# Attention into a mixture of experts and a gated layer: G's transfers moved to GpSimd's queue, XW written by VectorE, gate work re-ordered within a chunk

## The chip, the cores and the metric

The kernel runs on one core of one Trainium2 chip. Its time is the device time of one execution in microseconds. Before the change the median of three runs is 1039.93 us (1037.31 to 1040.97). The core's engines have queues of their own and meet at semaphores: TensorE (PE, matrix products into PSUM; PEld loads its weights), VectorE (DVE), ScalarE (ACT), GpSimd (POOL) and SyncE (SP). DMAs are issued from SP's queue (the profile calls it hardware_dynamic) and from GpSimd's (software_dynamic). Each queue is worked in order.

## The reference

Three layers follow one another, on 3072 tokens of 384 features (4 batches of 768 steps; 8 heads of 48).

```python
# 1: attention with a delta rule, state is 48x48 per batch and head
k_n = k / (norm(k) + 1e-6)
for t in range(768):
    y[:, :, t] = q_t @ state
    state = state + beta_t * outer(k_t, v_t - k_t @ state)
# 2: mixture of 8 experts, one per token
e = argmax(x @ w_gate); p = softmax(x @ w_gate)[e]
out = p * sigmoid(x @ w_output_gate)[e] * (relu(x @ w1[e]) @ w2[e])
# 3: gated layer
y = (sigmoid(x @ w_gate2) * (x @ w_val)) @ w_out
```

## The kernel before, in words

The kernel runs the layers as three stages. The first, attention, takes until about 304 us; the experts follow until about 570, and the gated layer until the end. The gate of the second layer (which expert each token gets, and its place in the list of that expert) is worked out during the first stage, for the tokens already finished, and their rows are scattered to the list `disp` in device memory by indirect DMAs on GpSimd's queue (`scatter`, L513).

The attention cuts the 768 steps into 12 chunks of 64, worked for all 32 pairs of batch and head at once. Inside a chunk the recurrence becomes a triangular system, solved in two halves of 32 rows with inverses of 32 x 32 blocks. Two chunks form a group, and a group's inverses are formed together: ScalarE copies the products of keys to `G` (diagonal blocks of a chunk's first half, rows of the tile `GD`) and to `GS`; two DMAs per chunk bring the second half's blocks from `GS` into `G` (`gp_evac`, L258; `G<-GS`). VectorE transposes `G` to `Lt` (`prep`), normalises, and builds the inverse `X` column by column (`inv_ops`: pairs of `tmp<-X,Lt` and `X<-X,tmp`). For groups 1 to 5 GpSimd does rows 16 to 30 of it (15 pairs `tmpG<-X,Lt`, `X<-X,tmpG`). The last step, `last`, transposes `X` to `XT`. Products need half of XT on other partitions; that is `XW` (`x_swap`, L271; `XW<-XT`).

The loop over chunks (L623 and after) then runs, for chunk c: the state read `KU<-SH,KQ` on TensorE; VectorE's first `W<-VT,KU`; the products with the inverse, `KU<-W,XT` and `KU<-W,XW` (64 small matmuls); ScalarE's copy `UF<-KU`; `KU<-UF,GS`; VectorE's second W; the inverse's products again; UF again; the state's update `Sps<-UF,KH`; and ScalarE's copy of the state to `SH`, from which the next chunk starts. Chunk 0 has no state, and its first products take `VT` in place of W. Beside this chain TensorE makes the products of keys for chunk c + 5 (`gp_mm`, `GY<-KQ`, in two halves), the output (`y_mm`: `GY<-SH,KQ`, and then `GY<-UF,PM`), and the gate's work on finished rows: transposes `XTP<-cst,XG` (`gate_t`), logits `GL<-wgo,xt` (`gate_l`, twice a chunk), and in odd chunks the places in the lists, `GL<-g_oh` and `GL<-acc,ones` (`gate_r`). VectorE does the small operations between them (`gate_v1`, `gate_e`, `gate_v2`).

VectorE's order is written out beforehand. `Filler` (L88) keeps a list of the inverse's steps (its main chain) and of side chains, each operation with an assumed duration. `fil.run(TA)` puts filler of a budget of TA between a chunk's first and second W, `fil.run(TB)` between the second W and the next chunk's first; `fil.add` hangs operations beside the main chain, `fil.flush(chain)` runs the filler until that chain is out, and the plain `flush(ops)` writes the operations out at once. At the end of an odd chunk the filler runs until the next group's inverse is done. `share_rows` hands out GpSimd's rows. SP's order is that of the code: at a chunk's end it loads V and K for chunk c + 2 (`VT`, `kt`, 8 transfers each), and fills part of `disp` with zeros.

Of the kernel before, what the change touches and what calls it, by code (L numbers as in the profile page):

```python
# [13 lines left out]
ALU = mybir.AluOpType  # L14
# [7 lines left out]
NSTEP, NG = SEQ // CH, SEQ // CH // 4  # L22
# [13 lines left out]
LA = 5  # L36
# [8 lines left out]
TC = 9.5  # L45
NR = 16
SHE = (0, 16, 16, 16, 16, 16)
TA = 6.0
TB = 11.0
TB0 = 11.0  # L50
W0 = 36
YS = 69
# [77 lines left out]
class Attention:  # L130
# [5 lines left out]
    def run(self, small, acc, zero_fill, small_loads):  # L136
# [121 lines left out]
        def gp_evac(c, k, ps):  # L258

            hs = slice(4 * k, 4 * k + 4)  # L260
            A.copy(out=gd(c)[:, :, hs], in_=ps[:, :, :, 0:32])
            A.copy(out=GS[c % RP][:, :, hs], in_=ps[:, :, :, 32:64])
            A.copy(out=PM[c % RP][:, :, hs], in_=ps[:, :, :, 64:128])
            if k:
                g, c2 = divmod(c, 2)
                for x in range(2):
                    SP.dma_start(
                        out=GD[g][quad(x, 1), 16 * c2 : 16 * c2 + 16].rearrange("p m t -> p (m t)"),
                        in_=GS[c % RP][quad(x, 1)].rearrange("p r h t -> p (r h t)"))

        def x_swap(g):  # L271
            x4 = XTS[g % 2].rearrange("p (c r h) t -> p c r (h t)", c=2, r=2)
            for x in range(2):
                o, i = XTW[g % 2][half(x)].rearrange("p c h t -> p c (h t)"), x4[half(1 - x), :, 1]
                if g:
                    SP.dma_start(out=o, in_=i)
                else:
                    V.tensor_copy(out=o, in_=i)

        def xt(c, h, b, i):  # L280

# [40 lines left out]
            sc = [(0.6, 0.0, lambda: scale(0, 16)), (0.33, GAP, lambda: scale(16, 32))]  # L322
            return ops, sc

        others, fresh = [], []

        def share_rows(n):
            for f in others[:n]:
# [4 lines left out]
        def inv_ops(g, share=32):  # L333

            X = ep.tile([128, 32, 32], F32, tag="X", name="X", bufs=2)

            def zero():
                (A if g else G).memzero(X.rearrange("p k i -> p (k i)")) if g else G.memset(X, 0.0)

            def diag(F):  # L340
                F.cut[g % 2] = 0
                if g:
                    others.extend(other)
                V.tensor_scalar_mul(out=X.rearrange("p k i -> p (k i)")[:, 0:1024:33], in0=nbr[:, g], scalar1=-1.0)
                F.t += 0.085
                F.ready = F.t + GAP

            def mul(E, j, k0, k1):
                n, m = k1 - k0, 31 - j
                tag, w = ("tmpG", 160) if E is G else ("tmp", 256)  # L350
                t = ep.tile([128, w], F32, tag=tag, name=tag, bufs=2)[:, : n * m].rearrange("p (a b) -> p a b", a=n)
                E.tensor_tensor(out=t, in0=X[:, k0:k1, j : j + 1].to_broadcast([128, n, m]), in1=LT[g][:, j : j + 1, j + 1 : 32].to_broadcast([128, n, m]), op=ALU.mult)
                return t

            def add(E, j, k0, k1, t):
                E.tensor_tensor(out=X[:, k0:k1, j + 1 : 32], in0=X[:, k0:k1, j + 1 : 32], in1=t, op=ALU.add)

            dur = lambda n, j: 0.095 + n * (31 - j) / 980

            def col(j):  # L360
                n = min(j + 1, share)

                def second(F, parts):
                    for k0, k1, t in parts:
                        add(V, j, k0, k1, t)
                        F.t += dur(k1 - k0, j)
                    F.ready = F.t + (GAP if len(parts) == 1 else 0.02)

                def first(F):
                    split = F.idle(F.t + dur(n, j)) and n * (31 - j) >= 100  # L370
                    if n // 2 - F.cut[g % 2] > CUT or not 0 < F.cut[g % 2] < n:
                        F.cut[g % 2] = n // 2
                    h = F.cut[g % 2]
                    ks = [(0, h), (h, n)] if split else [(0, n)]
                    parts = []
                    for k0, k1 in ks:
                        parts.append((k0, k1, mul(V, j, k0, k1)))
                        F.t += dur(k1 - k0, j)
                    F.ready = F.t + (0.0 if split else GAP)
                    if split:  # L380
                        second(F, parts)
                    else:
                        F.main.insert(0, lambda F: second(F, parts))

                return first

            def last(F):
                share_rows(99)
                V.transpose(out=XTS[g % 2].rearrange("p k i -> p i k"), in_=X.rearrange("p k i -> p i k"))
                F.t += 1.9  # L390
                F.ready = F.t
                F.done = g
                if g:
                    fresh.append(g)
                if g == 0:
                    V.memset(zl, 0.0)

            other = [(lambda j=j: add(G, j, share, j + 1, mul(G, j, share, j + 1))) for j in range(share, 31)]
            return zero, other, [diag] + [col(j) for j in range(31)] + [last]
# [6 lines left out]
        def GL(g):  # L406
            if not GLB:
                GLB.append(gp_.tile([128, 512], F32, tag="GL", name="GL", bufs=1))
            return GLB[0][:, 128 * (g % 2) : 128 * (g % 2) + 128]
# [92 lines left out]

        late = small["late"]

        def late_rows():

            tot = GL(NG - 1)[:, 96:97]
            raw_mm(out=tot, lhsT=ones, rhs=acc[:, 0:1], start=True, stop=True)
            V.tensor_scalar(out=late[:, 0:1], in0=tot, scalar1=-1.0, scalar2=float(E0), op0=ALU.mult, op1=ALU.add)
            V.tensor_scalar_max(out=late[:, 0:1], in0=late[:, 0:1], scalar1=0.0)  # L510
            V.tensor_copy(out=late[:, 1:8], in_=eoff[:, 1:8])

# [87 lines left out]
        ahead(3, ("GY", "KU"))  # L600
        ahead(4, ("GY", "KU"))
        k_turn(0)
        x_swap(0)
        ops, sc1 = prep(1)
        load_kq(LA + 1)
        for e in (1, 2):
# [16 lines left out]
        for c in range(NCH):  # L623
# [4 lines left out]
                early.close()  # L628

            beside(c, "load", engines)  # L630
            while fresh:
                x_swap(fresh.pop(0))
            S0, vp = SH, VT[c]
            KU = two("KU")
            KUv = KU[:, :, 0:384].rearrange("p r (h e) -> p r h e", h=8)
# [2 lines left out]
            Wv = W.rearrange("p r (h e) -> p r h e", h=8)  # L638
            sv = lambda b, h: S0[rows(b), pos(b), 48 * h : 48 * h + 48]

            def y_mm():
                for h, b in hb:
                    mm(out=Yp[half(pos(b)), par(b), 48 * h : 48 * h + 48], lhsT=kq(c, 1, h, b), rhs=sv(b, h), start=(h == 0), stop=False)

            if c > 0:
# [6 lines left out]
                    mm(out=KU[:, r, 0:384], lhsT=SHz[:, r, 0:128], rhs=SHz[:, r], start=True, stop=False)  # L652
                W1 = vp.rearrange("p r (h e) -> p r h e", h=8)
            if c % 2 == 1 and c > 1:
                fil.flush(fil.add(gate_v1(g - 1)))
            if more:
                P = gp_mm(c + LA, 0, "GY", mm)
            elif c > 0:
                Yp = two("GY")
                y_mm()  # L660
            beside(c, "KS", engines)
            if c > 0 and c + RK - 1 < NCH:
                load_kq(c + RK - 1)

            for h, b in sorted(hb, key=lambda x: par(x[1])) if c == 0 else hb:
                mm(out=KUv[quad(opp(b), 0), par(b), h], lhsT=xt(c, h, b, 0), rhs=W1[quad(pos(b), 0), par(b), h], start=True, stop=True)
            if c > 0:
                fil.run(TA)
            share_rows(NR // 2)
# [3 lines left out]
            if not last:  # L673
                v_mul(c + 1, (0,), A)
                vm = fil.add([(0.5, 0.0, lambda c=c: v_mul(c + 1, (1,), V))])
            if c % 2 == 1 and c > 1:
                gate_r(g - 1, mm)
                v2 = gate_e(g - 1) + gate_v2(g - 1)
            if c > 0:
                gate_t(2 * c - 2)  # L680
            if last:
# [2 lines left out]
                mm(out=KUv[quad(pos(b), 1), par(b), h], lhsT=GS[c % RP][quad(opp(b), 0), par(b), h], rhs=UF[quad(opp(b), 0), par(b), h], start=False, stop=False)  # L684
            V.tensor_tensor(out=W, in0=vp, in1=KU[:, :, 0:384], op=ALU.subtract)
            if c % 2 == 1 and c > 1:
                fil.flush(fil.add(v2))
                if last:
                    for j in range(2 * c - 6, 2 * c - 2):
                        scatter(j)  # L690
            if more:
                P = gp_mm(c + LA, 1, "GY", mm)
            if c > 0:
                gate_l(2 * c - 2, mm)
            if last:
                beside(c, "V", engines, Sps[:, 1])
            for h, b in hb:
# [3 lines left out]
            if more:  # L701
                gp_evac(c + LA, 1, P)
            if c > 0:
                gate_t(2 * c - 1)
            if not last:
                for h, b in hb:
                    mm(out=Sps[rows(b), pos(b), 48 * h : 48 * h + 48], lhsT=KH[c][half(opp(b)), par(b), h], rhs=UF[half(opp(b)), par(b), h], start=False, stop=False)
                SH = wk.tile([128, 2, 384], F32, tag="SH", name="SH", bufs=2)
                A.copy(out=SH, in_=Sps[:, :, 0:384])
# [13 lines left out]
                k_turn(c + 1)  # L723
            x_evac(c, Yp)
            if 3 <= c < NCH - 1:
                scatter(2 * c - 6)
                scatter(2 * c - 5)
            if c == NCH - 3:
                late_rows()
            beside(c, "rows", engines)  # L730
            if last:
                flush(gate_v1(g, 0, 2))
# [25 lines left out]
            fil.run((TB if more else TC) if c else TB0)  # L758
            share_rows(NR // 2)
            fil.flush(vm)  # L760
            if c2 == 1 and g + 1 < NG:
                while fil.done <= g:
                    fil.step()
                fil.until = max(fil.until, fil.t)
# [602 lines left out]
```

## Time and profile before

| | us |
|---|---|
| median of 3 runs | 1039.93 |
| profiled execution, whole | 1035.51 |
| its span, first to last instruction | 1033.8 |
| attention up to chunk 0's first product with XT | 0 to 46.9 |
| chunks 0 to 2 | 46.9 to 103.75 |
| chunks 2 to 10 (from first KU<-W to first KU<-W) | 103.75 to 271.59 |
| chunks 10 and 11 | 271.59 to 304.5 |
| experts | 304.5 to 570 |
| gated layer | 570 to 1033.8 |

The trace is one execution. "Busy" is the time in which an engine worked on an instruction; what stands in brackets behind an instruction in a timeline is the time in which its engine stood idle before it, and what ended that. The granted clock is a share of TensorE's upper level of 2.4 GHz; 0.50 is its lower level, 1.2 GHz. Over the whole span TensorE is busy 943.7 us and VectorE 504.8.

### The profile page before, as it was taken

To read this page: it belongs to the slowest core of one execution; us is meant where nothing else is said; L and a number is where in the kernel's file an instruction comes from. 1 tells how busy PE (TensorE), PEld (TensorE's weight loads), DVE (VectorE), ACT (ScalarE), POOL (GpSimd) and SP (SyncE) were. 2 spreads that over 40 slices of the span, in tenths; PEclk is the share of its full clock that TensorE was granted. 3 is DMA by queue.
4 is the path that set the end of the run, shared out by engine and by line. 5 is a ranking of instruction groups with operands and counts; after the bars stand their busy time and mean duration, and the time that the engine had idled before them with its cause. 6 is when DMAs were issued, how large, how long until landed. Compare 5 with 4: busy or idle time off the path is not lost. (4 is left out here: it accounts for less than half of the span.)

```text
span 1033.8 us, 24436 instructions
## 1 busy us (share of the span) xinstructions
PE 943.7 (91%) x10169; PEld 837.5 (81%) x10170; DVE 504.8 (49%) x1375; ACT 352.2 (34%) x693; POOL 328.4 (32%) x413
## 2 busy tenths in 40 slices
PE   6756878878889998998999999999999999999997
PEld 6655767768779887898899888888888888888886
DVE  6689978787245777677743754212112112111111
ACT  2532534434534544553554222212212112111111
POOL 3141350514132344444542233422322322322322
PEclk8755655555558999999999999999999999999999
DMA  5866463223433645565341311000000000000000
GB/s 128 154 177 178 106 126 78 79 73 82 140 103 104 223 131 156 165 200 174 108 145 48 79 61 46 31 1 1 31 1 1 31 1 1 31 1 0 31 1 32
DMA packets 64630, 84.19 MB, mean 81 GB/s; under 512 B 10473, under 2 KB 57074, under 8 KB 64514
## 3 DMA queue, kind: packets, MB, share of 16 engines
q1 hardware_dynamic: 61442, 73.11, 26.2%
q0 software_dynamic: 3072, 9.46, 2.5%
q8 instruction: 81, 1.33, 0.5%
q14 instruction: 35, 0.29, 0.1%
HBM read 64.13 MB, written 15.80 MB: 77 GB/s over the span
## 5 line engine op out<-in xcount | busy, mean ns | idle before, releaser
L1288 DVE TENSOR_TENSOR gf<-gf,g 128x512 f32<-128x512 f32 x72 | 49.4, 687 | 310.2 <-PE g L1280 309.6
L790 POOL TENSOR_TENSOR gsl<-gf,gsh 128x512 fp32r<-128x512 f32 x68 | 88.7, 1305 | 269.4 <-ACT gsh L789 269.2
L1287 ACT ACTIVATE gf<-g 128x512 f32<-128x512 f32 x72 | 43.0, 597 | 187.7 <-PE g L1280 184.0
L789 ACT CAST gsh<-gf 128x512 fp32r<-128x512 f32 x69 | 42.8, 621 | 144.5 <-DVE gf L1288 143.1
L1254 PE MATMUL o<-wol,gsh 128*128 128x384 f32 x272 | 87.1, 339 | 0.0
L1254 PE MATMUL o<-woh,gsl 128*128 128x384 f32 x272 | 86.6, 336 | 0.0
L76 DVE TENSOR_TENSOR X<-X,tmp 128x96 f32<-128x96 f32 (+42 forms) x286 | 69.6, 270 | 1.2
L76 DVE TENSOR_TENSOR tmp<-X,Lt 128x96 f32<-128x96 f32 (+42 forms) x286 | 68.9, 268 | 1.8
L970 DVE SCALAR_TENSOR_TENSOR hl<-h,hh 128x460 fp32r<-128x460 f32 (+7 forms) x57 | 33.1, 580 | 60.5 <-ACT hh L969 60.2
L1280 PE MATMUL g<-yl,wgh 128*128 128x512 f32 x216 | 62.5, 394 | 0.0
L1280 PE MATMUL g<-yl,wvh 128*128 128x512 f32 x216 | 62.4, 395 | 0.0
L929 PE MATMUL y<-hh,w2h 128*128 128x460 f32 (+6 forms) x168 | 60.8, 362 | 1.6 <-ACT hh L969 1.4
L1254 PE MATMUL o<-woh,gsh 128*128 128x384 f32 x272 | 62.2, 339 | 0.0
L1280 PE MATMUL g<-yh,wgh 128*128 128x512 f32 x180 | 60.7, 394 | 0.0
L76 ACT COPY UF<-KU 128x768 f32<-128x768 f32 x24 | 19.2, 799 | 120.5 <-PE KU L76 96.3
L929 PE MATMUL y<-hh,w2l 128*128 128x460 f32 (+6 forms) x168 | 58.5, 349 | 0.0
L76 PE MATMUL GY<-KQ 48*64 48x128 f32 (+1 forms) x640 | 44.5, 403 | 12.0 <-DMA KQ<-in_st_dram 12.0
L76 POOL TENSOR_TENSOR tmpG<-X,Lt 128x15 f32<-128x15 f32 (+7 forms) x90 | 33.4, 371 | 67.3 <-DVE X L76 60.7
L1254 PEld LDWEIGHTS o<-woh,gsh 128*128 128x128 f32 x272 | 49.7, 188 | 6.2
L1254 PEld LDWEIGHTS o<-wol,gsh 128*128 128x128 f32 x272 | 50.6, 188 | 2.4
L1280 PE MATMUL g<-yh,wgl 128*128 128x512 f32 x180 | 51.8, 394 | 0.0
L1280 PE MATMUL g<-yh,wvh 128*128 128x512 f32 x180 | 51.6, 394 | 0.0
(329 smaller groups left out, 2236.7 us busy)
## 6 DMA issues: line engine op xcount, KB each, us to landing
w1r<-in_w_dram SPq DMA_DIRECT2D x32, 384.0 KB
w2r<-in_w_dram SPq DMA_DIRECT2D x32, 384.0 KB
KQ<-in_st_dram SPq DMA_DIRECT2D x40, 192.0 KB
disp<-zrow SPq DMA_DIRECT2D x8, 772.0 KB
VT<-in_vtok_dram SPq DMA_DIRECT2D x96, 48.0 KB
kt<-in_ktok_dram SPq DMA_DIRECT2D x96, 48.0 KB
XG<-in_m2g_dram SPq DMA_DIRECT2D x12, 384.0 KB
XG<-in_m2v_dram SPq DMA_DIRECT2D x12, 384.0 KB
```

Source lines behind the costliest of these rows:

```text
L76: r = f(*args, **kw)
L789: (act or nc.scalar).copy(out=hi, in_=src)
L790: eng.tensor_tensor(out=lo, in0=src, in1=hi, op=ALU.subtract)
L929: self.T.matmul(out=ys[c][:, 0:n], lhsT=w2[l][:, f % 2, 128 * c : 128 * c + 128], rhs=(hh, hl)[r], start=(f == 0 and i == 0), stop=(f == 7 ...
L970: self.V.scalar_tensor_tensor(out=hl, in0=hp[:, 0:n], scalar=0.0, in1=hh, op0=ALU.max, op1=ALU.subtract)
L1254: T.matmul(out=ops_[m][:, 0:384], lhsT=gh[l][:, 128 * m : 128 * m + 128], rhs=wo[r][:, f], start=(f == 0 and i == 0), stop=(f == 11 and i ...
L1280: T.matmul(out=ps, lhsT=gv[w][l][:, c, 128 * f : 128 * f + 128], rhs=Y[r][c], start=(i == 0 and c == 0), stop=(i == 2 and c == 2))
L1287: A.activation(out=gf, in_=gps[0], func=AF.Sigmoid)
L1288: V.tensor_tensor(out=gf, in0=gf, in1=gps[1], op=ALU.mult)
```

## The change

The diff has four parts. The two `G<-GS` transfers of a chunk are issued by GpSimd in place of SP. `XW` is always written by two copies of VectorE, directly behind the transpose of `XT`, where before only group 0 did so and the others had SP transfers at the start of a chunk. The budgets of the filler go from 6.0 and 11.0 to 4.8 and 11.2. And the gate's work is re-ordered in a chunk: `gate_v1` is written out at once behind the first W; `gate_r` stands behind `KU<-UF,GS` in place of ahead of it; the first operation of `gate_v2`, which reads GL, is written out at once behind the second W and the rest goes into the filler until the scatter; the first `gate_l` stands behind the second `KU<-W` in place of ahead of it. Beside that chunk 0 makes its products with VT ahead of the key products, chunks from 7 on make `GY<-SH,KQ` in two halves, and `late_rows` is cut in a product on TensorE and three operations of VectorE.

```diff
-TA = 6.0
-TB = 11.0
+TA = 4.8
+TB = 11.2
@@ gp_evac
-                    SP.dma_start(
+                    G.dma_start(
                         out=GD[g][quad(x, 1), 16 * c2 : 16 * c2 + 16].rearrange("p m t -> p (m t)"),
@@ x_swap
-                if g:
-                    SP.dma_start(out=o, in_=i)
-                else:
-                    V.tensor_copy(out=o, in_=i)
+                V.tensor_copy(out=o, in_=i)
@@ inv_ops, last
                 F.done = g
-                if g:
-                    fresh.append(g)
-                if g == 0:
-                    V.memset(zl, 0.0)
+                x_swap(g)
+                F.t += 0.8
@@ late_rows
+        tot = []
+        def late_sum():
+            tot.append(GL(NG - 1)[:, 96:97])
+            raw_mm(out=tot[0], lhsT=ones, rhs=acc[:, 0:1], start=True, stop=True)
         def late_rows():
-            tot = GL(NG - 1)[:, 96:97]
-            raw_mm(out=tot, lhsT=ones, rhs=acc[:, 0:1], start=True, stop=True)
...
@@ the loop over chunks
             beside(c, "load", engines)
-            while fresh:
-                x_swap(fresh.pop(0))
...
             if c % 2 == 1 and c > 1:
-                fil.flush(fil.add(gate_v1(g - 1)))
-            if more:
+                flush(gate_v1(g - 1))
+            if more and c > 0:
                 P = gp_mm(c + LA, 0, "GY", mm)
             elif c > 0:
                 Yp = two("GY")
-                y_mm()
+                y_mm(hb[:16])
...
+            if c == 0:
+                P = gp_mm(c + LA, 0, "GY", mm)
             if c > 0:
                 fil.run(TA)
...
-            if c % 2 == 1 and c > 1:
-                gate_r(g - 1, mm)
-                v2 = gate_e(g - 1) + gate_v2(g - 1)
             if c > 0:
                 gate_t(2 * c - 2)
...
             V.tensor_tensor(out=W, in0=vp, in1=KU[:, :, 0:384], op=ALU.subtract)
             if c % 2 == 1 and c > 1:
-                fil.flush(fil.add(v2))
-                if last:
+                gate_r(g - 1, mm)
+                e = gate_e(g - 1)
+                v2 = gate_v2(g - 1)
+                flush(v2[:1])
+                v2 = e + v2[1:]
+                if c == NCH - 3:
+                    flush(v2)
+                    v2 = [0.0, []]
+                elif last:
+                    flush(v2)
...
+                else:
+                    v2 = fil.add(v2)
             if more:
                 P = gp_mm(c + LA, 1, "GY", mm)
-            if c > 0:
-                gate_l(2 * c - 2, mm)
+            elif c > 0:
+                y_mm(hb[16:])
...
             if c > 0:
+                gate_l(2 * c - 2, mm)
                 gate_t(2 * c - 1)
+            if c == NCH - 3:
+                late_sum()
...
             if 3 <= c < NCH - 1:
+                if c % 2 == 1:
+                    fil.flush(v2)
                 scatter(2 * c - 6)
                 scatter(2 * c - 5)
-            if c == NCH - 3:
-                late_rows()
...
             fil.flush(vm)
+            if c == NCH - 3:
+                late_rows()
```

On SP's queue the transfers stood between the loads. The piece of the difference on SP around chunks 0 to 2 (GS_110 to GS_113 belong to chunks 2 to 5, GS_108 and GS_109 to chunks 6 and 7; KQ, VT and kt are loads of inputs, zrow is the zero fill):

```order
-L76 DMA G<-GS_110 32x512 x2
-L76 DMA G<-GS_111 32x512 x2
-L76 DMA G<-GS_112 32x512 x2
 L76 DMA KQ_101<-in_st_dram 48x4x256 x4
 L76 DMA disp<-zrow 256x1x772 x2
-L76 DMA G<-GS_113 32x512 x2
 L76 DMA VT<-in_vtok_dram 32x384 x8
 L76 DMA kt<-in_ktok_dram 32x384 x8
 L76 DMA disp<-zrow 256x1x772 x2
 L76 DMA KQ_95<-in_st_dram 48x4x256 x4
-L76 DMA G<-GS_108 32x512 x2
```

They leave the queue altogether. On GpSimd they now stand among the row operations; the changed order there from the end of group 0's rows to the beginning of group 1's is:

```order
L76 TENSOR_TENSOR tmpG<-X,Lt 128x15
L76 TENSOR_TENSOR X<-X,tmpG 128x15
L76 DMA G<-GS_110 32x512 x2
L76 DMA G<-GS_111 32x512 x2
L76 DMA G<-GS_112 32x512 x2
L76 DMA G<-GS_113 32x512 x2
L76 TENSOR_TENSOR tmpG<-X,Lt 128x15
L76 TENSOR_TENSOR X<-X,tmpG 128x15
```

All four chunks' transfers stand ahead of group 1's first row; those of chunk 6 stand behind its last row, those of chunk 7 in the middle of group 2's rows, and those of chunk 8 behind them, ahead of the first scatters.

VectorE, at the end of chunk 1, where group 1's inverse ends and chunk 2's first W follows (XT_115 and XW_117 are the buffers of odd groups), as a piece of the difference:

```order
 L76 TENSOR_TENSOR X<-X,tmp 128x16
 L76 STREAM_TRANSPOSE XT_115<-X 128x32x32
+L76 COPY XW_117<-XT_115 64x512 x2
 L76 TENSOR_TENSOR W<-VT,KU 128x768
 L76 TENSOR_SCALAR X<-nbr 128x32
```

The two copies now stand between the transpose and W.

TensorE in chunk 3, behind the first products with the inverse (W, XT_115, XW_117), as a piece of the difference; lt and ones are constants, g_oh holds the experts that VectorE's gate_v1 has chosen:

```order
 L76 MATMUL KU<-W,XT_115 32x48
 L76 MATMUL KU<-W,XW_117 32x48
+L76 MATMUL XTP<-cst,XG 128x128 x3
+L76 MATMUL KU<-UF,GS_111 32x48 x32
 L76 LDWEIGHTS lt
 L76 MATMUL GL<-g_oh,lt 128x32
...
 L76 MATMUL GL<-acc,ones 128x32
-L76 MATMUL XTP<-cst,XG 128x128 x3
-L76 MATMUL KU<-UF,GS_111 32x48 x32
 L76 MATMUL GY<-KQ_96 64x128 x16
```

The rank products went behind KU<-UF,GS. The six `GL<-wgo,xt` that followed GY<-KQ_96 ahead of the second KU<-W now follow that, ahead of the next transposes.

## Rows read from the trace of the kernel before

**Rows 1.** The span cut by stage: stretch, length, busy us of each engine, granted clock.

```profile
103.75:271.59 167.84, 137.02 (x4192) 121.85 (x4192) 131.44 (x554) 73.46 (x166) 57.21 (x145) 0.57 0.39 94
...
304.50:570.00 265.50, 253.87 (x1496) 236.14 (x1494) 168.39 (x307) 125.05 (x235) 108.41 (x71) 0.97 0.46 142
570.00:1033.80 463.80, 455.91 (x2167) 396.07 (x2165) 109.32 (x178) 101.05 (x172) 128.14 (x107) 1.00 0.06 21
```

**Rows 2.** The same view, chunk 2 to 10, cut at each first KU<-W.

```profile
103.75:121.84 18.09, 17.77 (x536) 15.59 (x536) 17.30 (x61) 10.49 (x23) 8.10 (x24) 0.68 0.37 73
121.84:149.83 27.99, 18.57 (x553) 16.34 (x553) 23.44 (x107) 9.81 (x24) 11.76 (x32) 0.56 0.55 132
149.83:169.41 19.58, 19.12 (x537) 16.80 (x537) 13.65 (x47) 10.56 (x23) 3.36 (x7) 0.50 0.45 95
169.41:195.55 26.14, 18.93 (x558) 16.62 (x554) 22.65 (x106) 9.81 (x24) 9.86 (x25) 0.63 0.46 103
195.55:216.38 20.83, 18.88 (x569) 17.00 (x569) 14.29 (x56) 10.54 (x23) 5.61 (x14) 0.50 0.20 57
216.38:237.70 21.32, 15.15 (x483) 13.80 (x484) 18.12 (x95) 7.38 (x17) 6.90 (x20) 0.50 0.31 81
237.70:255.74 18.04, 15.45 (x481) 13.81 (x479) 17.27 (x69) 7.36 (x15) 7.96 (x19) 0.52 0.24 70
255.74:271.59 15.85, 13.15 (x488) 11.89 (x485) 4.72 (x22) 7.50 (x17) 3.67 (x7) 0.70 0.47 124
sum 167.84, PE 137.02 PEld 121.85 DVE 131.44 ACT 73.46 POOL 57.21; mean PE 17.13 PEld 15.23 DVE 16.43 ACT 9.18 POOL 7.15
```

**Rows 3.** Waits, 46.9 to 304.5 us: who, for whom, us in total, times, longest.

```profile
PE KU L76 <- DVE W L76: 17.4, 6, 6.9
DVE Lt L76 <- DMA G<-GS: 17.0, 3, 11.4
...
PE KU L76 <- DMA XW<-XT: 8.7, 6, 3.6
...
PE GL L76 <- DVE tmp L76: 4.5, 1, 4.5
...
PE GL L76 <- DVE g_c L76: 3.7, 2, 2.1
PE GL L76 <- DVE g_m L76: 3.2, 1, 3.2
PE GL L76 <- DVE g_oh L76: 3.2, 3, 1.7
```

**Rows 4.** Timeline of VectorE, chunk 0: start, us, instruction, idle before.

```profile
42.54 0.88 DVE L76 COPY XW<-XT 64x512 f32<-64x512 f32 x2
54.81 1.91 DVE L76 STREAM_TRANSPOSE Lt<-G 128x1024 f32<-128x1024 f32 x1 [11.39 <-DMA G<-GS]
...
59.03 0.95 DVE L76 TENSOR_TENSOR W<-VT,KU 128x768 f32<-128x768 f32 x1
```

**Rows 5.** Timeline of TensorE, chunk 0.

```profile
44.83 2.15 PE L76 MATMUL GY<-KQ 48*64 48x128 f32 x30 [0.43 <-DMA KQ<-in_st_dram]
...
50.28 1.50 PE L76 MATMUL KU<-UF,GS 32*32 32x48 f32 x64 [0.90 <-ACT UF L76]
```

**Rows 6.** Timeline of SP's queue, chunk 0.

```profile
49.61 4.96 SPq L76 DMA_DIRECT2D G<-GS  x6
```

**Rows 7.** Timeline of VectorE, first W of chunk 2.

```profile
100.41 0.95 DVE L76 TENSOR_TENSOR W<-VT,KU 128x768 f32<-128x768 f32 x1
```

**Rows 8.** GpSimd's groups by line, 46.9 to 304.5 us: busy us, mean ns.

```profile
L76 POOL TENSOR_TENSOR tmpG<-X,Lt 128x15 f32<-128x15 f32 (+7 forms) x75 | 28.5, 380 | 61.5 <-DVE X L76 56.0
...
L76 POOL DMA_INDIRECT disp<-XG,g_pos x20 | 20.8, 1040 | 35.1 <-DMA disp<-XG,g_pos 27.8 <-POOL XG L76 3.8 <-DVE tmp L76 2.3
```

**Rows 9.** DMA issues of the whole span: the scatters, us from issue to landing.

```profile
disp<-XG,g_pos POOLq DMA_INDIRECT x24, 3.0
```

**Rows 10.** Timeline of GpSimd in group 1's rows.

```profile
70.09 1.17 POOL L76 TENSOR_TENSOR tmpG<-X,Lt 128x63 f32<-128x63 f32 x1
```

More of the change, by code (lines that the diff above doesn't have):

```diff
@@ L323, in prep @@
             return ops, sc
-        others, fresh = [], []
+        others = []
         def share_rows(n):
@@ L503, in run @@
         late = small["late"]
+        tot = []
+        def late_sum():
+            tot.append(GL(NG - 1)[:, 96:97])
+            raw_mm(out=tot[0], lhsT=ones, rhs=acc[:, 0:1], start=True, stop=True)
         def late_rows():
-            tot = GL(NG - 1)[:, 96:97]
-            raw_mm(out=tot, lhsT=ones, rhs=acc[:, 0:1], start=True, stop=True)
-            V.tensor_scalar(out=late[:, 0:1], in0=tot, scalar1=-1.0, scalar2=float(E0), op0=ALU.mult, op1=ALU.add)
+            V.tensor_scalar(out=late[:, 0:1], in0=tot[0], scalar1=-1.0, scalar2=float(E0), op0=ALU.mult, op1=ALU.add)
             V.tensor_scalar_max(out=late[:, 0:1], in0=late[:, 0:1], scalar1=0.0)
@@ L602, in run @@
         k_turn(0)
-        x_swap(0)
         ops, sc1 = prep(1)
@@ L639, in run, with y_mm @@
             sv = lambda b, h: S0[rows(b), pos(b), 48 * h : 48 * h + 48]
-            def y_mm():
-                for h, b in hb:
+            def y_mm(hs=hb):
+                for h, b in hs:
                     mm(out=Yp[half(pos(b)), par(b), 48 * h : 48 * h + 48], lhsT=kq(c, 1, h, b), rhs=sv(b, h), start=(h == 0), stop=False)
```

## Prediction

> **What bounds the kernel now.** I read the stages first. From 570 us on TensorE is busy 455.91 of 463.80 us at a granted clock of 1.00, and the stage before it (304.5 to 570, granted clock 0.97) is just as dense, 253.87 of 265.50; the change moves nothing in either, so both should only start earlier. The steady stretch of the first stage, 103.75 to 271.59, is different: 137.02 of 167.84 at a granted clock of 0.57, which is mostly the lower of the two levels (1.2 GHz) [rows 1, 2]. The question is how much of its 31 idle microseconds, and of the start-up before it, goes.
>
> Second, the same stretch cut at the start of each chunk's first product with W, chunk 2 to chunk 10 [rows 2]. The steps alternate. Those that go from an odd chunk to the next even one (the 2nd, 4th and 6th row) last 27.99, 26.14 and 21.32 and leave TensorE idle for 27.99 - 18.57 = 9.42, 7.21 and 6.17: 22.8 together. The other five are idle for 0.32, 0.46, 1.95, 2.59 and 2.70, a mean of 1.6. Even these are at the lower clock, so a step costs about its TensorE work, near 18.9, plus a hand-over.
>
> Third, the waits of the stage [rows 3]. TensorE waits 17.4 for W, 8.7 for XW's DMA, and 4.5 + 3.7 + 3.2 + 3.2 = 14.6 in front of the gate products GL for VectorE's small gate operations; VectorE waits 17.0 for G, of which one wait is 11.4. XW and the gate together, 23.3, are about the idle time of the odd-to-even steps (a part of each belongs to the start-up and to the last chunks). So those steps are late because a gate read stands behind VectorE's filler and because SP issues the swap behind its loads, not because their work is longer.
>
> **The change, part by part.** *The start-up.* VectorE ends XW's copies at 42.54 + 0.88 = 43.42 and then stands 11.39 for G, because SP issues all six G transfers only at 49.61, behind loads and zero fills [rows 4, 6]. On GpSimd's queue the first four of them follow the last row operation of group 0, and their sources have long been copied, so at 1.04 us an issue and 3.0 to landing (the prices of the indirect scatters on that queue [rows 8, 9]; the nearest rows there are) they take 4 x 1.04 + 3.0 = 7.2 us and are there before 43.4 if they start by 36. VectorE's work from Lt to the first W is 59.03 - 54.81 = 4.22, so it could write W at 47.6. TensorE is not ready then: its inverse products now come first, at about 43.75; from there to the start of KU<-UF,GS it needs 3.30 (46.98 to 50.28), and the group products of 2.15 [rows 5] that used to stand ahead now fill the gap behind, ending near 48.4. With 1.50 for KU<-UF,GS that is 49.9, and W at 50.0 instead of 59.03: -9.0. Bounds: 0 if G lands where it does now, -11.4 if TensorE hid nothing.
>
> From there to chunk 2 VectorE does what it did, plus 0.88 for group 1's swap (two copies, as in group 0 [rows 4]) and a wait of perhaps 1.0 for group 2's G. Chunk 2's W comes at 100.41 - 9.0 + 0.88 + 1.0 = 93.3 [rows 7]. The products behind it ran freely only at 103.75, 3.3 after W began, since they waited for XW; with XW written by VectorE ahead of W they follow W by 1.0, so at 94.3. The start-up term is 94.3 - 103.75 = **-9.5**.
>
> *The odd-to-even steps.* Three edits act here and I price them together, as one idle time ends with the last of them. The swap: SP's issue and landing go, two copies come, and the copies stand ahead of W in VectorE's own order, so no wait for a DMA is left. The gate read: g_m<-GL is now the first thing behind the second W, and the products that overwrite GL have moved behind the second KU<-W, so when they come the read is 1.5 us old. The rank products: behind KU<-UF,GS, when gate_v1, written in one piece behind the first W, has had all of the first KU<-W, the UF copy and these products as cover. All three rest on one condition: that VectorE has less work in a step than TensorE. Its mean is 16.43 a step [rows 2]; with half a swap, 0.44, it is 16.9, under TensorE's 18.9. The new budgets (4.8 and 11.2) only cut this work elsewhere. So I let these steps look like the other five: 22.8 of idle become 3 x 1.6 = 4.8: **-18.0**. Bounds: 0 if something else ends last in the same place, -22.8 if nothing is left.
>
> *What is added.* The copies take VectorE 4 x 0.88 = 3.5 in the steps from chunk 2 to 10, at the one place where W stands behind them; I charge 1.5 of it, as VectorE has about 2 us of slack in a step. The halves of GY<-SH,KQ, the late sum and the missing MEMSET move work inside TensorE's and VectorE's slack: 0. The later G transfers (chunks 6 to 11) now stand in GpSimd's in-order queue among row operations and, from chunk 3 on, scatters. A row operation is 0.38 [rows 8], half a group of 15 pairs some 6 us, and G is wanted a chunk later. VectorE's waits for G beyond the first sum to 17.0 - 11.4 = 5.6 today [rows 3]; I leave that as it is: 0, with the bounds in the rivals. Sum: -9.5 - 18.0 + 1.5 = -26. The profiled execution took 1035.5 us (a span of 1033.8 and 1.7 around it) and would take 1009.5; it lies 4.4 under the median of the runs, 1039.9, so in the terms of the median the forecast is **1014**.
>
> **The rivals.** *B, G lands late.* GpSimd's operations stretch beside some VectorE work: a row of 63 elements takes 1.17 where the mean is 0.38 [rows 8, 10], a factor of 3.1. If issues stretch alike, a pair costs 2 x 1.04 x 3.1 = 6.4 and with landing 9.4 instead of 5.1. The start-up hardly feels it (VectorE stands still there, waiting for G, and stretches nothing), but three later groups would each wait up to 4.3 us more: 3 x 4.3 = +13, so 1027. For it: the row of 1.17. Against it: the scatters, issued while VectorE works, average 1.04 [rows 8], with no sign of two kinds; and a VectorE that waits for G no longer disturbs it.
>
> The Trainium skill has a sharper form of B: its page "SBUF — State Buffer", in the warning on the "DVE blocks DMA" trap, says that transfers issued from GpSimd get their descriptors from GpSimd itself, that it is shut out of a shared port while VectorE runs an fp32 copy from SBUF to SBUF, and advises the hardware queues; the page gives 620 ns alone against 3100 beside a copy. It speaks against this change, and the copies of the swap are of just that kind. The trace's 1.17 agrees that there is a lock of some sort, its scatters at 1.04 do not show a factor of 5; by the page's factor, as an estimate, a pair would cost 10.4 + 3.0, each of the three groups would be 8.3 late, and the sum would be -1: close to no change.
>
> *C, the denser TensorE is granted its upper clock.* In the first row of [rows 2] it was busy 17.77 of 18.09 and got a mean of 0.68, in the third 19.12 of 19.58 and got 0.50: dense steps get it sometimes. If it stayed up, VectorE would bind: 16.9 + 1.6 = 18.5 a step against 20.5, over six such steps -12, so 1002. Against it: one dense step after another is what the changed kernel has only if all hand-overs stay short.
>
> *F, nothing shifts.* The end of the odd chunk may wait for GpSimd's rows in place of the gates, and the experts' start for its weights: within 0.3% (3.1 us, about what a measurement of this kernel can tell from no change) of 1039. Against it: the start-up term is a single wait of 11.4 with nothing beside it.
>
> *E, slower.* GpSimd's rows are half of each group's inverse, and XT waits for both halves. If the new neighbours (the copies, and a VectorE that no longer pauses) stretch every row operation to 1.17, a group's 30 take 35.1 instead of about 15, and G for the next group stands behind them. Groups 2, 3 and 4 would each be late by up to 20, some 55 in all after slack; with the -26 that is +29, about 1068. It decides from a mean of 0.38 + 0.79 x 26/55 = 0.75 per row operation. Against it: the mean is 0.38 now, with VectorE busy 131 of 168 us.
>
> **How the numbers follow.** The forecast 0.57 (its own range 1007 to 1022: the start-up between -11.4 and -6, the steps between -22.8 and -12), B 0.17, C 0.13, F 0.05, E 0.08. Faster is the forecast, B and C: 0.87; within 0.3% F: 0.05; slower E: 0.08. The range leaves out E and F and the far side of C and B: 998 to 1034.
>
> **What would show it.** Right: VectorE's first Lt near 43.5 and W near 50; no DMA behind any first KU<-W; no wait of a microsecond in front of GL in chunks 3, 5 and 7; chunk-to-chunk steps of about 20 without the alternation; the experts starting near 278. B shows as waits of VectorE's Lt for G in chunks 2, 4, 6; C as a granted clock well over 0.57 between chunks 2 and 10; E as GpSimd rows of about a microsecond. The forecast is wrong if the alternation stays with other names in the waits.

## The result, and the profile after

The changed kernel takes 1011.39 us (median of four runs, 1010.09 to 1012.01) against 1040.45 for the kernel before in the same comparison: a ratio of 0.9722, 95% interval 0.9696 to 0.9748, or 29 us. Run again later beside other kernels it took 1014.71 (0.9749, 0.9726 to 0.9773). The traced execution took 1011.92 with a span of 1010.2, only 23.6 under the traced execution of before; that one (1035.51) lay 5 us under its own median, this one is at its median.

The steps from chunk 2 to chunk 10, cut as in [rows 2]; the columns are the stretch, its length, the busy time of PE, PEld, DVE, ACT and POOL, the granted clock, and the DMA share and GB/s:

```profile
94.34:113.97 19.63, 18.81 (x542) 16.64 (x542) 18.87 (x68) 10.58 (x23) 11.18 (x32) 0.50 0.54 124
113.97:134.14 20.17, 18.18 (x552) 15.99 (x548) 18.77 (x76) 9.86 (x24) 6.00 (x15) 0.67 0.53 115
134.14:153.63 19.49, 18.34 (x545) 15.92 (x542) 17.71 (x58) 10.58 (x23) 13.30 (x28) 0.59 0.61 123
153.63:174.16 20.53, 19.61 (x548) 17.31 (x548) 19.21 (x81) 9.85 (x24) 5.81 (x15) 0.50 0.30 84
174.16:194.60 20.44, 16.27 (x546) 14.24 (x543) 18.05 (x59) 10.48 (x23) 11.74 (x27) 0.75 0.24 67
194.60:213.04 18.44, 15.97 (x484) 14.03 (x484) 17.04 (x72) 7.61 (x17) 3.36 (x9) 0.50 0.25 69
213.04:230.06 17.02, 15.28 (x479) 13.71 (x479) 16.78 (x73) 7.28 (x15) 10.52 (x30) 0.50 0.21 59
230.06:246.92 16.86, 16.01 (x484) 14.35 (x484) 14.46 (x64) 7.63 (x17) 3.95 (x7) 0.50 0.35 90
sum 152.58, PE 138.47 PEld 122.20 DVE 140.90 ACT 73.87 POOL 65.87; mean PE 17.31 PEld 15.28 DVE 17.61 ACT 9.23 POOL 8.23
```

The alternation is gone: the 2nd, 4th and 6th step leave TensorE idle for 1.99, 0.92 and 2.47, where they left 22.8 together. The eight steps are 15.3 us shorter, at the same granted clock over the whole stretch (0.57 before and after). VectorE's work is spread more evenly: apart from the last step it lies between 16.78 and 19.21, where it lay between 13.65 and 23.44. With a mean of 17.6 in a step of 19.1 VectorE is now as near to the limit as TensorE.

How clear the alternation of before looks depends on the cuts. In [rows 2] chunks 2, 4 and 6 are cut where their products went on after waiting for XW. Their first products stand at 101.42, 145.20 and 191.75. Cut there, the steps of before are 20.42, 23.36, 24.21, 22.34, 24.63, 21.32, 18.04 and 15.85, because the wait for XW then counts for the even chunk's own step. The idle time is the same. By these cuts the start-up gave 7.1 us and the eight steps 17.6. A wait of before, and why it was there: XT for chunk 4 was ready at 136.2, and SP issued the swap 10.5 us later, behind its loads of V and K (three views):

```profile
134.13 2.06 DVE L76 STREAM_TRANSPOSE XT<-X 128x1024 f32<-128x1024 f32 x1 [0.48 <-DVE X L76]
```

```profile
142.59 3.96 SPq L76 DMA_DIRECT2D kt<-in_ktok_dram  x8
146.65 1.35 SPq L76 DMA_DIRECT2D XW<-XT  x2
```

```profile
149.18 0.28 PE L76 MATMUL KU<-W,XW 32*32 32x48 f32 x1 [3.61 <-DMA XW<-XT]
```

The waits of the first stage after the change (43 to 280 us), against [rows 3]: who waited for whom, us in total, times, the longest:

```profile
POOL G L76 <- ACT GS L76: 46.2, 5, 11.8
...
PE KU L76 <- DVE W L76: 18.4, 11, 7.8
...
DVE Lt L76 <- DMA G<-GS: 7.9, 4, 3.7
```

TensorE's entries for XW and for VectorE's gate operations, 23.3 us, are no longer among them. A new one leads: GpSimd stands for 46 us with a G transfer at the head of its queue whose source ScalarE has not copied yet.

The start-up on VectorE, which answers to [rows 4, 7]:

```profile
42.36 0.88 DVE L76 COPY XW<-XT 64x512 f32<-64x512 f32 x2
43.27 1.99 DVE L76 STREAM_TRANSPOSE Lt<-G 128x1024 f32<-128x1024 f32 x1
...
47.89 0.95 DVE L76 TENSOR_TENSOR W<-VT,KU 128x768 f32<-128x768 f32 x1 [0.39 <-PE KU L76]
...
59.95 2.04 DVE L76 STREAM_TRANSPOSE Lt<-G 128x1024 f32<-128x1024 f32 x1 [3.68 <-DMA G<-GS]
...
92.44 0.86 DVE L76 COPY XW<-XT 64x512 f32<-64x512 f32 x2
93.33 0.95 DVE L76 TENSOR_TENSOR W<-VT,KU 128x768 f32<-128x768 f32 x1
```

The wait of 11.39 is gone. W comes at 47.89, where it came at 59.03, and waits 0.39 for TensorE. A part is given back at the next group: its G, from chunk 5, makes VectorE stand for 3.68. TensorE starts chunk 2's products right behind W, with no wait for XW:

```profile
94.34 0.28 PE L76 MATMUL KU<-W,XT 32*32 32x48 f32 x1 [7.85 <-DVE W L76]
94.35 0.28 PE L76 MATMUL KU<-W,XW 32*32 32x48 f32 x1
```

### The profile page after: what moved, and what is told of

It is laid out like the page before. It is cut to its first block, busy times and chain, and to the rows that moved or that the text cites. A ratio compares the mean times of both kernels' runs of the same rounds, so it can differ in the third digit from the quotient of the medians.

```text
span 1010.2 us, 24422 instructions
## 1 busy us (share of the span) xinstructions
PE 943.6 (93%) x10169; PEld 836.4 (83%) x10170; DVE 512.8 (51%) x1358; ACT 352.9 (35%) x693; POOL 337.5 (33%) x433
## 5 line engine op out<-in xcount | busy, mean ns | idle before, releaser
L76 DVE TENSOR_TENSOR X<-X,tmp 128x160 f32<-128x160 f32 (+36 forms) x273 | 69.1, 278 | 1.6
L76 DVE TENSOR_TENSOR tmp<-X,Lt 128x160 f32<-128x160 f32 (+36 forms) x273 | 68.3, 275 | 2.2
L76 PEld LDWEIGHTS GY<-KQ 48*64 48x64 f32 x640 | 35.9, 205 | 20.1 <-issue 12.0
L1290 PE MATMUL g<-yh,wvl 128*128 128x512 f32 x180 | 51.6, 394 | 0.0
```

Of the source, the lines that this page charges most:

```text
L76: r = f(*args, **kw)
L1290: T.matmul(out=ps, lhsT=gv[w][l][:, c, 128 * f : 128 * f + 128], rhs=Y[r][c], start=(i == 0 and c == 0), stop=(i == 2 and c == 2))
```

## The experiments

Medians of one kernel vary from one comparison to another: the changed kernel's by 3.3 us, those of the kernel before by 6.3 (1035.63 to 1041.91). So beside each ratio stands a mark from the trace: the start of the first product with W in chunk 2 and in chunk 11. For the changed kernel the second mark is 262.4 in one trace and 262.8 in another; for the kernel before it is 288.6. (The 103.75 of the prediction is where chunk 2 went on after its wait for XW.) What lies behind the second mark, the rest of chunk 11, the experts and the gated layer, takes between 742.7 and 750.7 us in the fourteen traces, though the code of the two later stages is the same in all; this scatter is in the medians and not in the marks. Each mark is from one trace. Ratios are to the kernel before in the same comparison.

| kernel | chunk 2 | chunk 11 | median us | ratio (95% interval) |
|---|---|---|---|---|
| before | 101.4 | 288.6 | | |
| changed | 94.3 | 262.4 | 1011.39 | 0.9722 (0.9696 to 0.9748) |
| changed, again | 93.9 | 262.8 | 1014.71 | 0.9749 (0.9726 to 0.9773) |
| changed, G on SP | 102.9 | 266.8 | 1014.94 | 0.9822 (0.9793 to 0.9851) |
| changed, XW by transfer | 93.4 | 273.8 | 1023.11 | 0.9893 (0.9855 to 0.9931) |
| changed, gate order of before | 94.0 | 275.8 | 1025.12 | 0.9913 (0.9876 to 0.9949) |
| changed, budgets of before | 94.5 | 269.2 | 1018.49 | 0.9855 (0.9827 to 0.9883) |
| changed, chunk 0's order of before | 99.7 | 268.3 | 1019.00 | 0.9769 (0.9742 to 0.9796) |
| before, G on GpSimd | 98.3 | 281.5 | 1033.85 | 0.9928 (0.9902 to 0.9954) |
| before, XW by copies | 101.9 | 285.7 | 1033.87 | 0.9936 (0.9916 to 0.9957) |
| before, gate order | 100.5 | 284.0 | 1031.68 | 0.9900 (0.9857 to 0.9942) |
| changed, G on both queues | 97.0 | 263.5 | 1010.58 | 0.9696 (0.9665 to 0.9728) |
| changed, Lt later | 93.9 | 262.6 | 1012.85 | 0.9726 (0.9707 to 0.9746) |
| changed, both of these | 93.5 | 261.8 | 1011.16 | 0.9708 (0.9684 to 0.9732) |

The comparison with the undone parts G, XW, gate and budgets was one in which the kernel before was at 1035.63, 5 us under the others. The changed kernel was not run in it, so its ratios make these parts look 5 us dearer than their medians and marks do.

**G back on SP's queue.**

```diff
-                    G.dma_start(
+                    SP.dma_start(
```

> The changed kernel with one part undone: the G transfers go back to SP's queue, where the code issues them (behind loads and zero fills); all else as changed. Theory (three parts that add up; the start-up is G's alone): VectorE stands about 10 us for group 1's G again, the first W of chunk 0 moves from 47.9 to about 57 and chunk 2's first products from 94.3 to about 103; time 1011 + 9 = 1020. Rival (the start-up is won by chunk 0's new order, G would have come in time on SP as well once XW's transfers are gone): 1011 to 1014, no wait for G over 3 us in chunk 0.

Measured: chunk 2 comes 8.6 later, as the theory said, and VectorE stands for 11.95:

```profile
55.27 1.90 DVE L76 STREAM_TRANSPOSE Lt<-G 128x1024 f32<-128x1024 f32 x1 [11.95 <-DMA G<-GS]
...
59.49 0.96 DVE L76 TENSOR_TENSOR W<-VT,KU 128x768 f32<-128x768 f32 x1
```

But chunk 11 is only 4.4 late, and the time 1014.94 is under the 1020 expected; it lies 3.6 and 0.2 over the two medians of the changed kernel. The steps of chunks 2 to 10 take 148.06, not 152.58, and no later Lt waits for G. In the changed kernel three later ones do, for 0.28, 1.64 and 2.29. The second of them, from ScalarE's copy over GpSimd's queue to VectorE (three views):

```profile
142.61 0.39 ACT L76 COPY GS<-GY 128x256 f32<-128x256 f32 x1
```

```profile
143.76 0.35 POOL L76 TENSOR_TENSOR X<-X,tmpG 128x15 f32<-128x15 f32 x1
144.28 1.13 POOL L76 DMA_DIRECT2D G<-GS  x2 [0.17 <-issue]
```

```profile
147.48 2.01 DVE L76 STREAM_TRANSPOSE Lt<-G 128x1024 f32<-128x1024 f32 x1 [1.64 <-DMA G<-GS]
```

The copy ended at 143.0, and the transfers stood for 1.3 behind the last row operations of a group; on SP the same ones were issued as the copy ended. These waits, 4.2 together, would fit the 4.5, but the clock can have a share too: with G on SP the eight steps were granted 0.62 in place of 0.57, and TensorE's work in them is 132.4 and not 138.5. The third step was granted 0.97:

```profile
143.04:161.01 17.97, 15.37 (x546) 13.09 (x542) 17.83 (x58) 10.58 (x23) 11.68 (x28) 0.97 0.51 111
```

This row also shows what the upper level is worth here: TensorE's work falls to 15.4 (18.3 in the same step of the changed kernel, at 0.59), and the step is no shorter than VectorE's 17.83.

**XW by SP's transfers.**

```diff
-                V.tensor_copy(out=o, in_=i)
+                if g:
+                    SP.dma_start(out=o, in_=i)
+                else:
+                    V.tensor_copy(out=o, in_=i)
```

(and `x_swap` at the start of the even chunks again)

> The changed kernel with one part undone: XW of groups 1 to 5 is written by SP's transfers at the start of each even chunk again. Theory: TensorE's waits for that transfer come back, 8.7 us in six waits in the kernel before, less the copies of 0.88 that go from VectorE in four steps; time 1011 + 5 to 8 = 1016 to 1019, and the steps into chunks 4, 6 and 8 are the long ones. Rival (VectorE binds now, it is busy 17.6 of 19.1 us a step, so a copy that leaves it pays for the transfer): within 2 us of 1011.

Measured: 1023, 11 later at chunk 11, dearer than either had it. TensorE waits for the transfer by 12.8 us in all. The steps from chunks 2, 4 and 6, in which it is waited for, are longer by 2.8, 2.2 and 1.1; most of the cost is one wait in chunk 10:

```profile
258.41 0.28 PE L76 MATMUL KU<-W,XW 32*32 32x48 f32 x1 [8.25 <-DMA XW<-XT]
```

XT of that group was ready at 243.2, and SP issued the swap only after V's and K's loads and four loads of expert weights:

```profile
247.74 1.35 SPq L76 DMA_DIRECT2D kt<-in_ktok_dram  x3
...
251.82 1.40 SPq L76 DMA_DIRECT2D XW<-XT  x2
```

The rival falls: VectorE's copies are cheaper than the queue's delay although VectorE is nearly full. What the theory missed is that the delay moves. In the kernel before, SP issued the swaps for chunks 4, 6 and 8 between 10.5 and 12.0 us after their XT was ready, and here 0.4 to 2.3 us after. For chunk 10 it is the other way round. There the kernel before had its XT at 253.9, ahead of chunk 9's products, so that the swap was issued at once, a chunk ahead of its use. Here XT is ready only in the middle of chunk 9, and the swap stands behind the loads at the start of chunk 10. So 8.25 of the 11.4 is a wait that the kernel before did not have; about 3 remain for the others.

**The gate's order of before.** The edit puts back `fil.flush(fil.add(gate_v1(g - 1)))`, `gate_r` ahead of `gate_t`, the whole `gate_v2` in the filler, `gate_l` ahead of the second KU<-W and `late_rows` in one piece.

> The changed kernel with the gate's order undone: gate_v1 and gate_v2 interleaved with the filler, gate_r ahead of the first transposes, the first gate_l ahead of the second KU<-W, late_rows in one piece. Theory: TensorE waits in front of GL in chunks 3, 5 and 7 for about 4 us each again; time 1011 + 10 to 12 = 1021 to 1023, the steps from odd chunks long by that. Rival (the waits were where the swap's transfer waited too, and one is hidden in the other or in VectorE's load): 1011 + 4 or less.

Measured: 1025, chunk 11 13.4 later. TensorE's waits come back as named:

```profile
PE GL L76 <- DVE g_m L76: 13.0, 4, 4.9
...
PE GL L76 <- DVE g_oh L76: 4.4, 4, 1.3
```

The theory stands, a little above its range; the steps from chunks 3, 5, 7 and 9 are 23.55, 23.67, 21.70 and 20.87, longer by 3.1 to 4.0 each, and the others are within 0.6 of the changed kernel's.

**The budgets of before.**

```diff
-TA = 4.8
-TB = 11.2
+TA = 6.0
+TB = 11.0
```

> The changed kernel with the filler's budgets back at 6.0 and 11.0 (changed: 4.8 and 11.2), all else as changed. Theory: the budgets only move filler between the two halves of a step, 1.2 us from behind the second W to ahead of it: within 2 us of 1011. Rival (the even steps come from the budgets, which keep VectorE's work ahead of the second W short): TensorE waits for the second W by 1 us more in each of eight chunks, 1011 + 8 = 1019.

Measured: 1018.5, chunk 11 6.8 later: the rival. With more filler between the two W, VectorE comes late to the second one. The wait in front of it in chunk 7, first in the changed kernel and then with the old budgets:

```profile
201.50 0.28 PE L76 MATMUL KU<-W,XT 32*32 32x48 f32 x1 [1.58 <-DVE W L76]
```

```profile
207.69 0.28 PE L76 MATMUL KU<-W,XT 32*32 32x48 f32 x1 [3.51 <-DVE W L76]
```

In total TensorE's waits for W go from 18.4 to:

```profile
PE KU L76 <- DVE W L76: 30.7, 13, 8.7
```

**Each part alone, in the kernel before.** G on GpSimd (one word), XW by copies, and the gate's order.

> The kernel before with one part of the change alone: the G transfers on GpSimd's queue. In the runs so far the undone part gives two numbers: chunk 2 came 8.6 us later without it, and the eight steps after that were 4.5 us shorter (148.1 against 152.6), since G of later groups then no longer stands behind GpSimd's rows. Theory (the queue wins the start-up and loses some of it later): -6 to -7 at chunk 2 (chunk 0's order is the old one), +2 to +5 in the steps, 2 to 5 us faster than before. Rival (the loss in the steps comes from the swap's copies and the new gate order, not from the queue): 7 to 9 us faster.

> The kernel before with one part alone: XW always written by VectorE's copies behind the transpose of XT, no transfers of XW on SP. Theory (parts add): TensorE's 8.7 us of waits for XW go, 4 x 0.88 of copies come in the steps: 5 us faster than before. Rival (undone in the changed kernel it cost 1.0 to 2.4% by the ratios; if that is its worth alone too): 12 to 18 us faster. Rival 2 (VectorE's late gate reads in the same chunks hide it): within 3 us.

> The kernel before with one part alone: the gate's order of the changed kernel (gate_v1 written out behind the first W, gate_r behind KU<-UF,GS, the GL read behind the second W, the first gate_l behind the second KU<-W, late_rows in two parts); budgets 6.0 and 11.0, chunk 0 and GY<-SH,KQ as before. Theory (parts add): the waits in front of GL go, 10 to 13 us faster than before. Rival (VectorE's work at the end of the odd chunk only moves the wait to the first W of the even chunk): 5 us or less.

Measured: ratios of 0.9928, 0.9936 and 0.9900, which is 7.5, 6.7 and 10.4 us. By the marks at chunk 11 it is 7.1, 2.9 and 4.6. The first is the rival's: chunk 2 came 3.1 earlier and not 6 to 7, and the steps to chunk 10 lost nothing (165.6 from first product to first product, against 170.2), although later Lt again waited for G, by 3.12 and 0.56. The second is near the theory by its ratio and near its second rival by the mark. The third is at the theory's lower end by its ratio and inside the rival's range by the mark, so it stays undecided.

Do the parts add? By the marks the three alone give 14.6 of 26.2 us; by the ratios 24.6 of 27 to 29. Undone one at a time, the same three cost 4.4 + 11.4 + 13.4 at the mark, and with the budgets' 6.8 and chunk 0's 5.9 (below) 41.9, more than the whole change; by the medians the five cost between 27 and 44, according to which median of the changed kernel is taken. The budgets and chunk 0's order were not run alone, and of the XW part 8.25 is the wait that the kernel before did not have. So how far the parts are from adding up is not settled. What the trace does show, for XW, is how one wait can take another's place. The 8.7 us of waiting for XW went, and TensorE then waited more for the others (17.4 and 4.5 in [rows 3]):

```profile
PE KU L76 <- DVE W L76: 23.8, 9, 8.8
...
PE GL L76 <- DVE tmp L76: 7.5, 1, 7.5
```

**Chunk 0's order of before, and the changed kernel again.**

```diff
-            if more and c > 0:
+            if more:
                 P = gp_mm(c + LA, 0, "GY", mm)
...
-            if c == 0:
-                P = gp_mm(c + LA, 0, "GY", mm)
```

> The changed kernel with one part undone: chunk 0 makes its key products ahead of the products with VT again. Theory (with G early, TensorE is what the first W waits for): the first W of chunk 0 at 51 to 53 as with G's queue alone (53.3), against 47.9; chunk 2's first products 3 to 4 us later than 94.3; 1011 + 3 to 4. Rival (the wait of VectorE's second Lt for G takes it up, 3.7 there now): within 1.5 us of 1011, that wait at or near 0 and not longer.

> The changed kernel itself once more, beside the others of this call and beside the kernel before. Theory: its own time hardly depends on the occasion (1011, within 3), so that the medians of the undone parts may be set against 1011: G on SP +4, XW by transfer +12, gate order +14, budgets +7. Rival (the chip of the first experiments was faster by the 5 us by which the kernel before was, 1035.6 against 1040.5, and the undone parts cost 5 us more than that): a ratio of 0.972 in every call, whatever the medians.

Measured: 1019.0 beside 1014.7, and W of chunk 0 at 53.80, waiting for TensorE:

```profile
53.80 0.95 DVE L76 TENSOR_TENSOR W<-VT,KU 128x768 f32<-128x768 f32 x1 [5.89 <-PE KU L76]
```

The theory holds in kind, with 5.4 to 5.9 in place of 3 to 4 at chunk 2: the key products in front also wait for their load (1.36 in that trace). With G early, more than half of the start-up's gain hangs on this order. The changed kernel's own time was 3.3 over its first, with the kernel before at 1041.91: neither "the same ratio" nor "the same median" is quite so, and single microseconds can't be read from either.

**Two attempts to go further.** G on both queues, `(G if c <= LA else SP).dma_start(`, that is by GpSimd for chunks 2 to 5 and by SP after; the waiting time ahead of group 2's preparation, `WP`, 12.0 in place of 6.0 in chunk 0; and both.

> The changed kernel with the G transfers of chunks 2 to 5 on GpSimd's queue (as changed) and those of chunks 6 to 11 on SP's (as before). Theory (GpSimd's queue is right only at the start, where SP is full of loads; later G stands behind GpSimd's rows and VectorE's Lt waits for it): chunk 2's first products at 94 as in the changed kernel, the steps to chunk 10 148 as with all G on SP, no wait of Lt for G in chunks 2, 4 and 6: 4 to 5 us under the changed kernel, a ratio to before near 0.968. Rival (the shorter steps of that run were the clock's, granted 0.97 in one step, and not the queue's): the ratio of the changed kernel, 0.972 or above, and steps of 152.

> The changed kernel with one number changed: the waiting time that the filler assumes ahead of group 2's preparation, 12.0 in place of 6.0, only in chunk 0. VectorE's second Lt then stands behind chunk 1's first W. Theory (the 3.7 us for which VectorE stands there, waiting for chunk 5's G, lie on the path to chunk 2): the wait is gone, chunk 2's first products at 90 to 91 in place of 94.3, 1011 - 3 to 4. Rival (in chunks 0 and 1 GpSimd's rows or the 28 us of VectorE's own work set the end): chunk 2 at 93 to 95, no change.

> Both at once: G of chunks 2 to 5 on GpSimd's queue, of chunks 6 to 11 on SP's, and 12.0 ahead of group 2's preparation. Theory: chunk 2 at 91 to 92, the steps from there to chunk 10 149 to 151, no wait of Lt for G over 1 us; 4 to 6 us under the changed kernel in this call. Rival (later G on SP arrives no sooner than on GpSimd's queue when VectorE comes earlier): the time of the kernel with the waiting time alone.

Measured: none can be told from the changed kernel. G on both queues (1010.58, in a comparison without the changed kernel) lost 2.6 at chunk 2, where Lt waited for 5.1 instead of 3.7. Its later Lt had no wait for G, and yet its steps took 151.0 and not 148, so the 148.06 was not the queue's alone. With the longer waiting time alone the rival holds: VectorE's second Lt stands behind chunk 1's first W and has no wait for G, but the second W behind it waits for TensorE:

```profile
65.70 1.93 DVE L76 STREAM_TRANSPOSE Lt<-G 128x1024 f32<-128x1024 f32 x1
...
69.43 0.95 DVE L76 TENSOR_TENSOR W<-VT,KU 128x768 f32<-128x768 f32 x1 [1.51 <-PE KU L76]
```

and chunk 2 comes at 93.9, as in the second trace of the changed kernel. Both together took 1011.16, ratio 0.9708 (0.9684 to 0.9732), against 0.9749 (0.9726 to 0.9773) beside it: 3.6 us by the medians, with intervals that overlap a little. Its chunk 2 came at 93.5 and its steps took 152.7, where 91 to 92 and 149 to 151 were expected, and its chunk 11 is only 0.6 to 1.0 earlier. That it is faster is not shown.

## Why the prediction was right, step by step

*The whole.* 1014 was forecast and 1011.4 and 1014.7 were measured. The mechanism is the one that the traces show: TensorE's waits for XW's transfer and for the gate operations are gone, and so is VectorE's long wait for G; put back one at a time, each brought its wait back. The closeness of the number has some luck in it. Up to chunk 11 the traces gained 9.4 + 15.3, and 1.5 more in chunk 10, which no term had: 26.2, where the sum was 26.

*The start-up, -9.5.* From 103.75 to 94.34, -9.4, but by two errors that cancel. The first W came at 47.89 and not at 50.0: TensorE was granted 1.00 there and made the products with VT and the key products in 3.5 us together, where the products with VT and the wait behind them had taken 3.37 alone, at 0.51:

```profile
43.39 0.31 PE L76 MATMUL KU<-VT,XT 32*32 32x48 f32 x5
...
46.89 0.88 PE L76 MATMUL KU<-UF,GS 32*32 32x48 f32 x64
```

And group 2's G made VectorE wait for 3.68, not the 1.0 that was allowed.

*The odd-to-even steps, -18.0.* Their idle time is 5.4 where 4.8 was forecast: -17.4. Their length fell by 16.3 (75.5 to 59.1), since TensorE's work in them grew by 1.1, and the other five steps grew by 1.0. All eight together gave 15.3, where -18.0 + 1.5 = -16.5 had been set.

*VectorE's load.* The condition that it has less work than TensorE in a step did not hold: 17.6 and not 16.9, against TensorE's 17.3. The margin of 2 us was never there: 16.9 is a mean over all eight steps, and it was set beside the 18.9 of the longer ones, while TensorE's mean over the eight was 17.13 [rows 2]. The gain came all the same, because both engines still fitted into 19.1. Of the 9.5 us by which VectorE's busy time rose the copies are 3.5. Its instructions overlap, and their lengths added up rose only from 169.2 to 172.5; so the rest is less overlap and not more work.

*The budgets.* The step that failed: that they "only cut this work elsewhere", at no cost. Undone, they cost 6.8 at chunk 11. The total came out right because it was set by the idle time that should be left, not by adding up parts, and what the budgets had to do for that was hidden in it.

*The queue.* G on GpSimd was issued in about half a microsecond, not 1.04, and took longer to land, 5.0 and not 3.0. The 5.0 is rough: the trace has a landing for four of the twenty transfers only (2.3, 4.1, 5.9 and 6.5). The lines give nanoseconds least, median and most, and then the view's last line:

```profile
L76 POOL DMA_DIRECT2D G<-GS x20: 496/538/770, 30.3 to 184.8; - x20
...
DMA to landing us min/median/max: 2.3/5.0/6.5
```

So B's mechanism, issues stretched threefold, is not there. Its sign did show: VectorE's Lt waited for G in chunks 2, 4 and 6. But these waits are 4.2 together, and in the kernel before VectorE stood for 8.4 in front of the same three (0.69 and 4.87 for G, 2.86 for ScalarE). The warning of the Trainium skill ("SBUF — State Buffer", the "DVE blocks DMA" trap) was hardly put to the test: VectorE was at work beside all twenty issues, but only one of them, the second of the pair at 41.64, stood beside copies of XW. It took 0.76, no longer than the first of all, which had none beside it (0.77), and SP's own took 0.59 in the median. Whether the time to landing is descriptors written late, or DMA engines that are busy otherwise, no run here separates. What the trace does show is simpler: in three of the ten pairs the transfers stood for 1.3 to 2.8 us behind row operations, as GpSimd works its queue in order.

*The other rivals.* C did not come true: the stretch was granted 0.57, as before. Single steps got more (0.67, 0.59 and 0.75, and 0.97 in one of another run), as single steps of before had. E did not either: the row operations kept their lengths (0.34 in the mean, for 0.38 and 0.33 before). The row of 1.17 that B and E start from is one of five such rows among thirty; the same shape took 0.31 just ahead of it. The experts' first products came 26.9 earlier than before (280.6 for 307.5), where 26.5 was forecast. The stretch behind chunk 11 became 2.6 longer (745.2 to 747.8); this lies within the scatter of all traces (742.7 to 750.7). The halves of GY<-SH,KQ, which the prediction set at 0, were not undone by any run.

## What to carry to other kernels

Where several short waits stand beside one another in a step, price the step by the idle time that a good step of the same kernel leaves, not wait by wait. With XW's wait of 8.7 taken away alone, other waits of the kernel before grew by 9.4 and chunk 11 came only 2.9 earlier; and a wait put back into the changed kernel can come back larger and elsewhere (8.25 in chunk 10). Whether parts add up can't be told where the times and the marks of single traces differ as much as here. A transfer belongs on the queue that has nothing in front of it at that moment; the same move to another queue gained 8.6 us at one place and brought waits of 1.6 and 2.3 at others, whose cost in time is not shown. When an engine's work is laid out by assumed durations, the numbers of that layout are part of the change and need a price of their own.

## What was not expected of the hardware

A plain 64 KB transfer from tile to tile took GpSimd no longer to issue (0.54 us) than SP (about 0.59), though GpSimd's indirect scatters take 1.04. A step in which TensorE was busy for 19.61 of 20.53 us was granted 0.50, the lower level, and another, busy for 15.37 of 17.97, was granted 0.97: in these steps the busier one did not get the higher clock.
